# Fused linear attention and GEGLU block: a new partition layout for q, k and v, and kv on quarters of the array

## The chip, the cores and the metric

The kernel runs on one core of a Trainium2 chip. The core has a matrix engine (TensorE, PE in the profile, with PEld for its weight loads), VectorE (DVE), ScalarE (ACT), GpSimd (POOL), SyncE (SP, which issues DMAs) and 16 DMA engines. The metric is device time in microseconds (us). PE writes to PSUM, which has eight banks of 128 x 512 f32; the other engines read the results from there.

## The reference

The inputs are q, k, v of shape 8 x 8 x 576 x 64 (batch, head, token, width) and three weights, all f32.

```python
q_s = softmax(q over the last axis); k_s = softmax(k over the tokens)
kv  = einsum('bhsd,bhse->bhde', k_s, v)            # 64 x 64 per head
o   = einsum('bhsd,bhde->bhse', q_s, kv)
x   = o.transpose(0, 2, 1, 3).reshape(4608, 512)
out = (gelu(x @ w_gate) * (x @ w_val)) @ w_out     # 512 -> 1536 -> 512
```

The kernel takes no maximum off before the exponentials, works in f16 between f32 sums, and divides kv by the sum of exp(k) after the matmul.

## The kernel before, in words

**Layout.** With nine tokens to a group, a head is 64 groups of nine. Partition 2m+t holds group m: for t = 0 tokens 0 to 4, for t = 1 tokens 5 to 8 with an unused slot in front, which is filled once with a value whose exponential is zero (k) or with zero (v). So a tensor of a batch is a tile of 128 partitions x 8 heads x 5 slots x 64, 2560 elements to a partition, of which a tenth is the unused slot. `load` (L180) issues two DMAs for a tensor, one for each t, from SP; in batch 0 the second goes from ACT's queue. `exp` (L223) writes exponentials in f16 as slot x head x width; `cast_v` (L232) makes v f16 and puts a column of ones behind every head.

**Attention of a batch.** `norm_sum` (L241) and `norm_pair` (L250) sum exp(q) over the width on DVE, `norm_mul` (L263) multiplies by the reciprocal on DVE or POOL. q is transposed by PE in batches 0 and 1 (`unit_t`, L391, eight 128x128 transposes for two pairs of heads, twice a batch, copied from PSUM by DVE) and by a DMA from batch 2 on (`unit_td`, L415). kv of a pair of heads is a sum of five matmuls, one for each slot. Batch 1 (`kv_mm`, L304) computes a 128 x 130 block per pair, of which the two blocks off the diagonal are masked away; batch 0 (`kv0_mm`, L340) and the others (`unit_kv4`, L361) compute the two heads of a pair as two matmuls with 64 columns of weights, 40 matmuls a batch. In batch 0 the sums of exp(k) come from matmuls against a column of ones (`ksum_mm`, L327), since k lands before v. x = q_s kv is one 128x128 matmul of 512 columns per pair in batches 0 and 1 (`unit_x`, L438) and eight 64x64 matmuls on quarters of the array in the others (`unit_x4`, L454). The 64 tokens of each batch that don't fit into its 512 are gathered over all batches into a ninth piece of work.

**The block.** Batches 0 and 1 compute twelve slices (fi) of 128 of the 1536 inner columns: four matmuls of 512 columns for gate (psg) and four for val (psv) each, Gelu on ACT, the product on DVE (`ffn_fi`, L520). The first slices are interleaved with the last of the attention (`ffn_first0`, L551; `ffn_first`, L527). The output of batch 0 is plain (`mm_out`, L577, four row tiles, psy). The output of batch 1 (`out_strassen`, L756) and both stages of the rest use Strassen's seven products of half matrices, which need sums of weights and of activations: `sum_w`, `sum_wgv`, `sum_h`, `sum_x`, on DVE and POOL. Weights come through six staging tiles in column chunks (`WCH`, L48), gate and val alternating, and are cast to f16 by POOL (`cast_w`, L209).

**Order.** Every engine and queue executes in program order. For batches 0 and 1 the order is the code's own from L1001 on, with `plan` (L1059) hanging attention steps of the next batch behind slices and output tiles. From batch 2 on it is written out in `PROG` (L675) as words: `0P1` a product, `K` the kv matmuls of the next batch, `k` their normalisation, `X` its x matmuls. PSUM banks go round in a ring (`big`, L81): six and two small ones at first, eight from batch 2 on; a matmul that takes a bank waits for the last reader of it. At the start PE multiplies a constant (`warm_pe`, L500, tile pswarm) until data is there.

Of the kernel before, what the change touches and what calls it, by code (L numbers as in the profile page):

```python
# [18 lines left out]
def kernel(  # L19
# [23 lines left out]
    NM = 4  # L43
    NC = NM + 1
    MAIN = NM * P
    REM = S - MAIN
    VW = D + 1
    WCH = [0, 128, 256] + list(range(512, F + 1, 256))  # L48
    NW = len(WCH) - 1
# [69 lines left out]
    mask = const.tile([P, 2, D], f32)  # L119
# [3 lines left out]
    for i in range(2):  # L123
        eq_b.append(const.tile([P, NC, C], f16, name=f"eq{i}"))
    ek_b.append(const.tile([P, NC, C], f16, name="ek"))
    v16_b.append(const.tile([P, NC, H, VW + 1], f16, name="v16"))
# [5 lines left out]
    eq0r = const.tile([P, C], f16)  # L132
    ld_b = {nm: [const.tile([P, H, NC * D], f32, name=f"{nm}t{i}") for i in range(n)]
# [11 lines left out]
    q0r = [x[0:64].rearrange("p (h d) -> p h d", d=D) for x in (  # L145
        kt1[:, 36 * P:].bitcast(f32), eq_b[1].rearrange("p n c -> p (n c)").bitcast(f32)[:, 1024:])]
# [4 lines left out]
    nc.vector.memset(ld_b["k"][0][:, :, 0:D], -1e30)  # L151
    nc.vector.memset(ld_b["v"][0][:, :, 0:D], 0.0)
    nc.vector.memset(tiny, 0.0)
    nc.vector.memset(ones, 1.0)
    nc.vector.memset(mask, 0.0)
    nc.vector.memset(mask[0:64, 0, :], 1.0)
    nc.vector.memset(mask[64:128, 1, :], 1.0)
    nc.vector.memset(ld_b["q"][0][:, :, 0:D], 0.0)
    make_identity(nc, ident)
    nc.gpsimd.memset(v16_b[0][:, :, :, D:D + 1], 1.0)  # L160
    nc.gpsimd.memset(ld_b["k"][1][:, :, 0:D], -1e30)
# [8 lines left out]
    QUAD = 2  # L170

    def heads(x, b, h0, h1):

        if b >= QUAD:
            return x.rearrange("p (t c) x -> p c t x", t=2)[:, h0 // 2:h1 // 2]
        return x[:, h0:h1]

    tiles = {}

    def load(src, nm, b, h0, h1, n0):  # L180
        tiles[(nm, b)] = buf(ld_b[nm], b)
        for t, c0 in ((0, n0), (1, 1)):
            (nc.scalar if b == 0 and t == 1 else nc.sync).dma_start(  # L183
                out=tiles[(nm, b)][t:P:2, h0:h1, c0 * D:NC * D],
                in_=src[b, h0:h1].rearrange("h (m n) d -> m h (n d)", n=NT)[
                    :, :, (4 * t + c0) * D:(4 * t + NC) * D])

# [6 lines left out]
    def load_w_gv(c):  # L194
        for w, nm in ((moe_w_gate, "wg"), (moe_w_val, "wv")):
            t = wst_tile(f"{nm}st", HP, WCH[c + 1] - WCH[c])
            nc.sync.dma_start(
                out=t, in_=w.rearrange("(ci p) f -> p ci f", p=P)[:, :, WCH[c]:WCH[c + 1]])
            wst[(nm, c)] = t
# [9 lines left out]
    def cast_w(nm, c, eng="pool"):  # L209
        dst = (wg_sb if nm == "wg" else wv_sb)[:, :, WCH[c]:WCH[c + 1]]  # L210
        copy_on(eng, dst, wst[(nm, c)])

    def load_w_o(c):
        t = wst_tile("wost", 2, C)
        nc.sync.dma_start(
            out=t, in_=moe_w_out.rearrange("(fi p) m -> p fi m", p=P)[:, 2 * c:2 * c + 2, :])
        wst[("wo", c)] = t

    def cast_w_o(c, eng="pool"):
        copy_on(eng, wo_sb[:, 2 * c:2 * c + 2, :], wst[("wo", c)])  # L220


    def exp(nm, b, h0=0, h1=H, n0=0):  # L223
        dst = ek_b[0] if nm == "k" else buf(eq_b, b)
        o, i = (("p n (c t d) -> p c t n d", "p c t (n d) -> p c t n d") if b >= QUAD else
                ("p n (h d) -> p h n d", "p h (n d) -> p h n d"))
        nc.scalar.activation(  # L227
            out=dst[:, n0:NC, h0 * D:h1 * D].rearrange(o, d=D, **({"t": 2} if b >= QUAD else {})),
            in_=heads(tiles[(nm, b)], b, h0, h1)[..., n0 * D:NC * D].rearrange(i, d=D),
            func=ACTF.Exp)  # L230

    def cast_v(b, h0, h1, eng="pool"):  # L232
        if h1 - h0 > 2 and (eng == "pool" or b >= QUAD):
            for h in range(h0, h1, 2):
                cast_v(b, h, h + 2, eng)
            return
        copy_on(eng, v16_b[0][:, :, h0:h1, 0:D].rearrange("p n h d -> p h n d"),
                (tiles[("v", b)][:, h0 // 2::4] if b >= QUAD else tiles[("v", b)][:, h0:h1]).rearrange(
                    "p h (n d) -> p h n d", d=D))

    def norm_sum(b, hp, n0=0):  # L241
        n = NC - n0
        e = buf(eq_b, b)[:, n0:NC, hp * P:(hp + 1) * P].rearrange("p n (h d) -> p n h d", d=D)
        rq = att.tile([P, n, 2], f32, name="rq", tag="rq", bufs=4)
        nc.vector.reduce_sum(rq, e, axis=mybir.AxisListType.X)
        rrq = att.tile([P, n, 2], f32, name="rrq", tag="rrq", bufs=4)
        nc.vector.reciprocal(out=rrq, in_=rq)
        st[(b, "norm", hp)] = (e, rrq, n)

    def norm_pair(b, g, n0, engs):  # L250

        n = NC - n0
        e = buf(eq_b, b)[:, n0:NC, 2 * g * P:(2 * g + 2) * P].rearrange("p n (h d) -> p n h d", d=D)
        rq = att.tile([P, n, 4], f32, name="rq2", tag="rq2", bufs=2)
        nc.vector.reduce_sum(rq, e, axis=mybir.AxisListType.X)  # L255
        rrq = att.tile([P, n, 4], f32, name="rrq2", tag="rrq2", bufs=2)
        nc.vector.reciprocal(out=rrq, in_=rq)
        for j in range(2):
            st[(b, "norm", 2 * g + j)] = (e[:, :, 2 * j:2 * j + 2], rrq[:, :, 2 * j:2 * j + 2], n)
        for j, eng in enumerate(engs):  # L260
            norm_mul(b, 2 * g + j, eng)

    def norm_mul(b, hp, eng="dve"):  # L263
        e, rrq, n = st[(b, "norm", hp)]
        (nc.gpsimd if eng == "pool" else nc.vector).tensor_tensor(  # L265
            out=e, in0=e, in1=rrq.unsqueeze(-1).to_broadcast((P, n, 2, D)), op=ALU.mult)

    def norm_mul2(b, hp, cut):
        e, rrq, n = st[(b, "norm", hp)]
        for eng, r in ((nc.vector, slice(0, cut)), (nc.gpsimd, slice(cut, n))):  # L270
            eng.tensor_tensor(out=e[:, r], in0=e[:, r], in1=rrq[:, r].unsqueeze(-1).to_broadcast(
                (P, r.stop - r.start, 2, D)), op=ALU.mult)

    def norm(b, hp, eng="dve", n0=0):
        norm_sum(b, hp, n0)
        norm_mul(b, hp, eng)

    def load_rem0():
        for h0 in (0, 4):
            nc.sync.dma_start(out=q0r[h0 // 4], in_=q[0, h0:h0 + 4].rearrange(  # L280
                "h (m n) d -> m h (n d)", n=NT)[:, :, 0:D])

    def exp_rem0():
        for i in range(2):
            nc.scalar.activation(
                out=eq0r[0:64, i * 4 * D:(i + 1) * 4 * D].rearrange("p (h d) -> p h d", d=D),
                in_=q0r[i], func=ACTF.Exp)

    def norm_rem0():
        e = eq0r[0:64].rearrange("p (h d) -> p h d", d=D)  # L290
        rq = att.tile([64, H], f32, name="rq0", tag="rq0", bufs=1)
        nc.vector.reduce_sum(rq, e, axis=mybir.AxisListType.X)
# [881 lines left out]
```

## Time and profile before

| what | time or share |
|---|---|
| time, median of 3 runs (lowest to highest) | 288.78 us (288.78 to 289.06) |
| profiled execution, first to last instruction | 286.9 us |
| PE busy | 277.9 us, 97% |
| DVE busy | 248.3 us, 87% |
| ACT busy | 209.8 us, 73% |
| POOL busy | 137.9 us, 48% |
| first matmul of the block (psg) starts | 14.96 us |
| slice 2 of batch 0 starts | 19.59 us |
| batch 0's slices end | 36.85 us |
| batch 1's slices end | 70.84 us |
| batch 2's first product starts | 82.11 us |

The profile has the execution's own time as its span alone; the timed median is 1.9 us above the span, for what lies before the first and after the last instruction. All windows and starts are counted from the first instruction. In a timeline a row is a run of equal instructions with its start, its length and, in brackets, how long the engine was idle before it and what ended that. A matmul's row reaches to the modelled end of the last one in it, some 0.2 us after the next row's start, so distances are taken from start to start. The granted PE clock is 1.00 throughout.

### The profile page before, as it was taken

Reading aid. Unit: us, or ns where it says so; the run is one execution under the profiler, and the core shown is the slowest. Engines: PE = TensorE matmul, PEld = TensorE weight load, DVE = VectorE, ACT = ScalarE, POOL = GpSimd, SP = SyncE. Lnnn points to the kernel's source line nnn. Section 1 sums busy time; section 2 is a strip of 40 time slices with the busy share of each in tenths; the row PEclk is TensorE's granted clock in tenths of the full one; section 3 lists DMA queues with packets and bytes.
Section 4 is the critical chain, followed back from the end, with each engine's and each line's share of the span. In section 5 each row is a group of like instructions: output and inputs, shape, how many; then the busy total and the mean of one; then the engine's idle time right before and its main releaser. Section 6 shows DMA issues by size and latency. Waiting matters only on the chain.

```text
span 286.9 us, 6704 instructions
## 1 busy us (share of the span) xinstructions
PE 277.9 (97%) x2581; PEld 216.4 (75%) x2581; DVE 248.3 (87%) x497; ACT 209.8 (73%) x370; POOL 137.9 (48%) x128
## 2 busy tenths in 40 slices
PE   3999999999999999999999999999999999999994
PEld 1544445445888888888888888888888888888883
DVE  2854788877999999979989998999999799998993
ACT  3773367884798889978998899799794577716740
POOL 1557845987339721865864258542553104110110
PEclk9999999999999999999999999999999999999999
DMA  6999999999139916159149853690304030003303
GB/s 215 375 380 386 401 393 390 394 328 243 35 139 339 258 34 223 78 101 321 45 98 308 289 164 150 182 249 2 147 6 90 0 150 0 2 0 77 73 2 146
DMA packets 54623, 51.74 MB, mean 180 GB/s; under 512 B 18496, under 2 KB 50496, under 8 KB 54592
## 3 DMA queue, kind: packets, MB, share of 16 engines
q1 hardware_dynamic: 52864, 49.49, 54.0%
q10 hardware_dynamic: 1728, 1.84, 2.0%
q8 instruction: 20, 0.33, 0.5%
q14 instruction: 11, 0.09, 0.1%
HBM read 37.75 MB, written 9.44 MB: 164 GB/s over the span
## 4 chain that ended last, share of the span: by engine, by line
PE 91%; DVE 5%; ACT 1%; issue 1%; ACTq 1%; DVEq 0%
PE psa L670 24%; PE psc L670 12%; PE psA L749 12%; PE psg L511 7%; PE psv L511 7%; PE psC L749 6%; PE psb L670 6%; PE psy L579 4%; PE psB L749 3%; PE pswarm L503 2%; PE pskv L368 1%; PE psa L749 1%; DVE rq L255 1%; ACTq L183 1%; DVE yo L770 1%
## 5 line engine op out<-in xcount | busy, mean ns | idle before, releaser
L670 PEld LDWEIGHTS <-wgv_sb 128*128 128x128 f16 x672 | 65.7, 98 | 8.0 <-issue 0.3
L265 POOL TENSOR_TENSOR eq<-eq,rrq 128x640 f16<-128x640 f16 (+1 forms) x27 | 34.9, 1303 | 24.3 <-ACT psb L858 11.7
L749 PEld LDWEIGHTS <-ht 128*128 128x128 f16 x384 | 37.2, 98 | 5.3 <-issue 0.4
L670 PE MATMUL psa<-xs,wgv_sb 128*128 128x256 f16 x288 | 40.4, 273 | 0.1
L511 PEld LDWEIGHTS <-wgv_sb 128*128 128x128 f16 x192 | 18.6, 98 | 21.9 <-issue 0.2
L858 ACT COPY psb<-psa 128x512 f32<-128x512 f32 x42 | 24.2, 583 | 8.3 <-PE psa L670 8.1
L511 PE MATMUL psv<-xt,wgv_sb 128*128 128x512 f16 x96 | 26.6, 379 | 0.0
L511 PE MATMUL psg<-xt,wgv_sb 128*128 128x512 f16 x96 | 26.6, 379 | 0.0
L516 ACT ACTIVATE gl<-psg 128x512 f32<-128x512 f32 x24 | 13.8, 597 | 16.7 <-PE psg L511 16.7
L517 DVE SCALAR_TENSOR_TENSOR ht<-psv,gl 128x512 f16<-128x512 f32 x24 | 16.1, 686 | 10.5 <-PE psv L511 8.7
L839 ACT ACTIVATE snq<-psc 128x512 f32<-128x512 f32 x35 | 20.6, 602 | 5.7 <-PE psc L670 5.6
L227 ACT ACTIVATE ek<-kt 128x1280 f16<-128x1280 f32 (+1 forms) x11 | 19.2, 1758 | 5.9 <-DMA kt<-in_k_dram 4.2
L670 PE MATMUL psb<-xt,wgv_sb 128*128 128x256 f16 x144 | 21.6, 273 | 0.0
L670 PE MATMUL psa<-xt,wgv_sb 128*128 128x256 f16 x144 | 21.0, 273 | 0.0
L255 DVE TENSOR_REDUCE rq<-eq 128x20 f32<-128x1280 f16 (+1 forms) x12 | 17.1, 1424 | 4.4 <-ACT eq L227 4.4
L749 PEld LDWEIGHTS <-sh 128*128 128x128 f16 x192 | 18.6, 98 | 2.8 <-issue 0.4
L749 PE MATMUL psA<-tw,ht 128*128 128x256 f16 x168 | 20.6, 272 | 0.0
L227 ACT ACTIVATE eq<-qt 128x2560 f16<-128x2560 f32 (+2 forms) x10 | 18.4, 1861 | 2.6 <-DMA qt<-in_q_dram 2.6
L886 POOL TENSOR_TENSOR ht<-cc 128x512 f16<-128x512 f32 x12 | 15.3, 1274 | 9.1 <-ACT cc L884 8.8
L876 DVE SCALAR_TENSOR_TENSOR ht<-psb,gl 128x256 f16<-128x256 f32 x42 | 17.1, 412 | 1.8 <-ACT gl L874 1.6
L874 ACT ACTIVATE gl<-psa 128x256 f32<-128x256 f32 x42 | 16.1, 385 | 3.4 <-PE psa L670 2.9
L874 ACT ACTIVATE gl<-psb 128x256 f32<-128x256 f32 x42 | 15.5, 382 | 3.8 <-PE psb L670 3.4
(192 smaller groups left out, 694.8 us busy)
## 6 DMA issues: line engine op xcount, KB each, us to landing
out_dram<-yo SPq DMA_DIRECT2D x15, 512.0 KB, 3.5
kt<-in_k_dram SPq DMA_DIRECT2D x7, 640.0 KB, 8.3
vt<-in_v_dram SPq DMA_DIRECT2D x7, 640.0 KB, 7.2
qt<-in_q_dram SPq DMA_DIRECT2D x7, 640.0 KB, 7.0
qt<-in_q_dram SPq DMA_DIRECT2D x8, 512.0 KB, 7.5
wost<-in_moe_w_out_dram SPq DMA_DIRECT2D x6, 512.0 KB, 7.9
kt<-in_k_dram SPq DMA_DIRECT2D x6, 512.0 KB, 7.4
vt<-in_v_dram SPq DMA_DIRECT2D x6, 512.0 KB, 6.6
```

What stands on the lines that cost most here:

```text
L227: nc.scalar.activation(out=dst[:, n0:NC, h0 * D:h1 * D].rearrange(o, d=D, **({"t": 2} if b >= QUAD else {})), in_=heads(tiles[(nm, b)], b, ...
L255: nc.vector.reduce_sum(rq, e, axis=mybir.AxisListType.X)
L265: (nc.gpsimd if eng == "pool" else nc.vector).tensor_tensor(out=e, in0=e, in1=rrq.unsqueeze(-1).to_broadcast((P, n, 2, D)), op=ALU.mult)
L511: nc.tensor.matmul(ps, w[:, ci, fi * P:(fi + 1) * P], xt[:, ci, :], start=(ci == 0), stop=(ci == HP - 1))
L517: nc.vector.scalar_tensor_tensor(out=ht[:, fi, :], in0=psv, scalar=_H_SCALE, in1=gl, op0=ALU.mult, op1=ALU.mult)
L670: nc.tensor.matmul(ps[:, t], a, x, start=(first and t == 0 and c == 0), stop=(c == 1), skip_group_check=True)
L749: nc.tensor.matmul(ps[t], a, w, start=(first and j == js[0] and (t == ts[0] or ps[t].tensor is not ps[ts[0]].tensor)), stop=(j == js[-1]), ...
L839: nc.scalar.activation(out=dst, in_=src, func=ACTF.Copy, scale=scale)
L858: nc.scalar.copy(out=t[f"b{k}"], in_=t[f"a{k}"])
L874: nc.scalar.activation(out=gl, in_=t[ps][:, 1], func=ACTF.Gelu)
L876: nc.vector.scalar_tensor_tensor(out=ht[:, k if x[2] == "2" else k + NO // 2, 0:256], in0=t[ps][:, 0], scalar=_H_SCALE, in1=t["g" + ps], o ...
L886: (nc.vector if side == "dve" else nc.gpsimd).tensor_tensor(out=ht[:, k:k + NO // 2 + 1:NO // 2, 256:512], in0=cc[:, :, 0], in1=cc[:, :, 1 ...
```

## The change

A pair of heads now lies on the two halves of the partitions: partition 64 hh + m holds group m of heads 2a + hh, a = 0 to 3, with all nine tokens: 4 x 9 x 64 = 2304 elements, no unused slot. A tensor is one DMA from SP (batch 0, and k and v of batch 1: two, by halves of a, called j). Exponentials, sums and products go by j or a.

```diff
-    def load(src, nm, b, h0, h1, n0):
+    def load(src, nm, b, j0=0, j1=2, n0=0):
...
-        for t, c0 in ((0, n0), (1, 1)):
-            (nc.scalar if b == 0 and t == 1 else nc.sync).dma_start(
...
+        nc.sync.dma_start(
+            out=tiles[(nm, b)][:, 2 * j0:2 * j1, n0 * D:NT * D],
+            in_=bass.AP(tensor=base.tensor, offset=base.offset + 4 * j0 * S * D + n0 * D,
+                        ap=[[NT * D, P], [2 * S * D, 2 * (j1 - j0)], [1, (NT - n0) * D]]))
...
-    WCH = [0, 128, 256] + list(range(512, F + 1, 256))
+    WCH = [(0, 256, 0, 2), (0, 256, 2, 4), (256, 512, 0, 4), (512, 768, 0, 4)] + [
+        (c, c + 384, r, r + 2) for c in (768, 1152) for r in (0, 2)]
```

The weight chunks are (columns, rows of 128): the first 256 columns come by halves of the rows, the last two 384 columns by halves. The fills of the unused slots and the mask are gone from the start of DVE and POOL.

kv of all batches goes on four 64x64 quarters of the array: the row half is the head of the pair (hh), the column half the slot of the pair (t), and nine tokens are summed. The two row halves write to two PSUM banks, in `unit_kv4` too.

```diff
+    def quarters(j):
+        for hh in range(2):
+            for t in range(2):
+                yield 2 * j + t, hh, t, slice(64 * hh, 64 * hh + 64), slice(64 * t, 64 * t + 64)
...
+    def kv_mm(b, j):
+        for n in range(NT):
+            for a, hh, t, r, o in quarters(j):
+                nc.tensor.matmul(st[(b, "pskv")][hh][o, j, 0:D], ek_b[0][r, n, a * D:(a + 1) * D],
+                                 v16_b[0][r, n, a, 0:D], start=(n == 0), stop=(n == NT - 1))
...
+    def x_mm(b, j, ps, src):
+        for a, hh, t, r, o in quarters(j):
+            nc.tensor.matmul(ps[t][r], st[(b, "kv")][o, hh, j, :], src(b, j, t, hh), start=True, stop=True)
```

`ksum_mm` is 36 such matmuls of one column per j, `unit_kv` (batch 1) and `unit_kv4` 72 of 65 columns a batch. x of batches 0 and 1 is `x_mm`, eight quarter matmuls of 512 columns instead of four full ones. `t_mm` and `t_out` are the transposes and their copy. `kv_norm` scales by the reciprocal, one row half on DVE and one on ACT; `kv4_norm` takes two reciprocals and two products instead of one each.

The start of batch 0 and the slices of batches 0 and 1:

```diff
-    warm_pe(15)
-    unit_t(0, 0, None)
...
+    warm_pe(14)
+    t_mm(0, 0)
+    kv_banks(0)
+    ksum_mm(0, 0)
+    t_out(0, 0, "act")
+    ksum_rec(0, 0)
+    cast_vn(0, 0, (0, 3, 6, 9), ("dve", "act", "pool"))
     warm_pe(3)
...
+    ksum_mm(0, 1)
+    ksum_rec(0, 1)
+    t_mm(0, 1)
+    kv_mm(0, 0)
+    t_out(0, 1, "dve")
+    kv_norm(0, 0, ("dve", "act"))
+    cast_vn(0, 1, (0, 3, 6, 9), ("dve", "act", "pool"))
+    unit_x(0, 0, True)
+    kv_mm(0, 1)
...
+    first = [((L(kv_norm, 0, 1, ("dve", "dve")), L(unit_x, 0, 1, True), L(preload, ACTF.Gelu)), ()),
+             ((), ())]
...
+            ffn_first(xt, (0, 1), first[b])
...
+                for fis in ((2, 3), (4, 5), (6, 7, 8), (9, 10, 11)):
+                    ffn_group(xt, fis)
```

The new `ffn_first` runs, for slices 0 and 1, gate and then val on rows 0 and 1, what `first` holds between them, and then rows 2 and 3. The new `ffn_group` runs the gate of all slices of a group and then their val. In the queue of SP, k and v of batch 1 come as k, k, v, v, and the second half of the last chunk of w_out behind them. In batch 0's output the last slice (11) of all four row tiles comes after slices 0 to 10 of all four, and the attention of batch 1 hangs there:

```diff
+    at(0, NS, 15, L(t_mm, 1, 1), L(t_out, 1, 1, "dve"), L(cast_vn, 1, 0, (0, 4, 9), ("dve", "act")))
+    at(0, NS, 16, L(cast_vn, 1, 1, (0, 4, 9), ("dve", "act")),
+       L(load_batch, 2, ((v, "v"),)))
+    at(0, NS, 17, L(kv_banks, 1), L(unit_kv, 1), L(cast_w_o, 5, "pool", 1, 2))
+    at(0, NS, 6, L(unit_x, 1, 0, True), L(unit_x, 1, 1, False, ()), L(sum_w, 3, "pool"))
+    at(0, NS, 8, L(x_out, 1, 1), L(sum_w, 1), L(sum_w, 2, "pool"), L(exp, "q", 2), L(preload, ACTF.Gelu))
...
-    at(1, NS, 2, L(sum_wgv, "g", 3), L(sum_wgv, "v", 3))
+    at(1, NS, 0, L(sum_wgv, "g", 3, 0, NO // 2, "pool"), L(sum_wgv, "v", 3, 0, NO // 2, "pool"))
```

Two sums of weights (`sum_wgv`, 3) thus move from DVE to POOL in batch 1's output. `PROG` is unchanged; only its words' contents shrink from 2560 to 2304 elements a tensor.

## The prediction

> **What bounds the kernel now.** First the page's head and its table of busy time.
>
> ```profile
> span 286.9 us, 6704 instructions
> ...
> PE 277.9 (97%) x2581; PEld 216.4 (75%) x2581; DVE 248.3 (87%) x497; ACT 209.8 (73%) x370; POOL 137.9 (48%) x128
> ```
>
> PE is busy 97% of the span. Second, the table by stage (length, busy time and count of PE, PEld, DVE, ACT, POOL, then clock, DMA share, GB/s), since 97% of the whole does not say where the rest lies.
>
> ```profile
> 14.96:19.59 4.63, 4.63 (x35) 1.93 (x30) 1.88 (x5) 3.73 (x7) 3.17 (x4) 1.00 1.09 383
> ...
> 70.84:82.11 11.27, 11.12 (x151) 9.09 (x149) 11.07 (x23) 8.93 (x9) 3.36 (x4) 1.00 0.23 84
> 82.11:287.00 204.89, 200.96 (x2052) 176.14 (x2050) 187.58 (x386) 158.52 (x307) 87.34 (x76) 1.00 0.42 127
> ```
>
> From 19.59 on PE has nothing to wait for: the psg and psv rows follow each other by 0.86 us per four matmuls (0.216 each), products of 256 columns by 1.31 per twelve (0.109 each). The one exception is batch 1's output, 70.84 to 82.11, where DVE is busy 11.07 of 11.27. So time can be won in three places: before 19.59, in PE's own work, and in that output. Third, the chain of waits at the start, and ACT's timeline under it.
>
> ```profile
> 4.91 5.95 PE pswarm L503 x15
> ...
> 13.16 0.34 PE pskv L346 x10
> ...
> 15.03 0.32 PE psg L511
> ...
> 19.59 0.86 PE psg L511 x4
> ```
>
> ```profile
> 6.52 2.00 ACT L227 ACTIVATE eq<-qt 128x1024 f16<-128x1024 f32 x2 [1.67 <-DMA qt<-in_q_dram]
> 10.02 2.43 ACT L227 ACTIVATE ek<-kt 128x1280 f16<-128x1280 f32 x2 [1.50 <-DMA kt<-in_k_dram]
> 12.57 1.45 ACT L205 CAST v<-vt 128x320 f16<-128x320 f32 x3
> ...
> 17.31 1.28 ACT L506 ACT_TABLE_LOAD   x1
> ```
>
> ACT waits for the whole of q, then of k, then of v: the start is bound by transfers. Fourth, PE's timeline around kv and x, for what a quarter of the array costs.
>
> ```profile
> 45.56 0.74 PE L309 MATMUL pskv<-v,ek 128*128 128x130 f16 x10
> 46.13 1.03 PE L579 MATMUL psy<-wo_sb,ht 128*128 128x512 f16 x4
> ...
> 101.69 0.82 PE L368 MATMUL pskv<-v,ek 128*64 128x65 f16 x40
> 102.45 0.50 PE L749 MATMUL psB<-wo_sb,ht 128*128 128x256 f16 x3
> ...
> 106.48 0.26 PE L462 MATMUL psxr<-eqt,kv 64*64 64x64 f16 x8
> 106.56 0.60 PE L462 MATMUL psx<-eqt,kv 64*64 64x512 f16 x8
> 107.10 1.26 PE L749 MATMUL psC<-wo_sb,s 128*128 128x256 f16 x10
> ```
>
> From start to start, batch 2's kv holds PE 0.76, one half of batch 1's 0.57, eight quarter matmuls of 512 columns 0.54, eight of 64 columns 0.08. Eight times 512 columns one by one would be 8 x 0.216 = 1.73: four quarters run together.
>
> **The change, part by part.** The sum is made against the profiled span of 286.9; the runs' median of 288.78 is 1.9 above it, and I add the same.
>
> *Start of batch 0.* The bytes of q, k, v are the same, but come in order by halves. ACT's half of q (0.52 MB) landed 4.4 us after its issue at 0.73, so q's first half is there at 5.1, the second at 6.4 (SP's half took 5.7). At 0.386 MB/us (5 to 12.4 us) each further 0.59 MB takes 1.53: k at 7.9 and 9.5, v at 11.0 and 12.5. That one queue starts as fast as two is not shown; if it doesn't, up to 0.5 is lost, and rows of 2304 bytes instead of 1024 and 1280 may win as much (402 GB/s were moved from 37 to 40 us, with rows up to 2 KB). I take neither. SP issues six DMAs of 0.8 (its rows are 0.76 to 0.92), done by 5.5, ahead of the transfers; the weights queue behind them as before. ACT is freed of three issues, so its table load and the warm-up start 2 us sooner. ACT then does exp q 5.1 to 6.2 (1.0 each), exp q 6.4 to 7.5, exp k (1152 elements, 1.15 from the 1.27 for 1280) 7.9 to 9.1 and 9.5 to 10.7, the transposed q (1024 elements, 1.0 as for exp) to 11.7, its third of v (0.46, as for 320 elements) to 12.2. DVE's sums, reciprocals and products (1.22 + 0.25 + 0.69 after each exp q) are done by 10.6, POOL's two products of 1.5 by 11.5, both ahead of ACT. So kv starts at 12.2 instead of 13.16. Its nine steps, kv's scaling (0.35 before, taken the same), x (0.4) and the copy (0.59, behind ACT's third of v's second half) put the first psg at 14.3 instead of 14.96. From there to slice 2 before took 4.63: sixteen matmuls (3.45), two x, two kv. After, it is sixteen matmuls and one x by quarters, 0.5 with its switch of array mode: 18.3. There slice 2's gate needs the bank of slice 0's, whose Gelu waits for the copy of x, the table load (1.28 + 0.20) and itself (0.60): 18.4. **-1.2.**
>
> *Weights.* Nobody waits for them now. Slice 4's gate weights are the tightest:
>
> ```profile
> 20.94 1.04 POOL L203 CAST wgv_sb<-wgst 128x1024 f16<-128x1024 f32 x1 [1.58 <-DMA wgst<-in_moe_w_gate_dram]
> ```
>
> They are cast at 21.98; after, PE wants them at 18.4 + 3.45 = 21.85, with the same bytes ahead. The chunks of 512-byte rows are gone (347 GB/s from 12.4 to 15.0 against 385 after it), which brings 0.3. So nothing is lost here, with 0.2 to spare; without that cover 0.1 is. The later groups need larger chunks at once (0.79 MB, 2.0 us, cast in two parts of 0.8), but their group of three gives PE 5.2 us for 4.0 of transfers.
>
> *Batch 1's attention.* PE's work: kv 2 x 0.57 becomes 0.70 (below), x 4 x 0.216 = 0.86 becomes 0.54: -0.75. The price is late work. PE reaches kv at 36.85 - 1.2 + 44 x 0.216 + 0.9 for the transposes = 46.0. The last transfer of v, issued at 41.1, landed at 47.1 before (6.0); k, k, v, v with half a w_out chunk moved behind (0.26 MB, 0.65 us), the 0.3 from above and a cast of 0.7 (640 elements) on two engines at once put v at 46.2 landed, 46.9 cast; larger rows could bring 0.8. PE waits 0 to 0.9: I take 0.4. Behind that wait stand slice 11 of the output, for which its weights come another 0.65 + 0.61 (a 512-element cast) after v's landing, 47.5, and x. Then x's copies (0.59, 0.69) come before batch 1's first psg, with only one row tile (0.22) to cover them: 0.5. Last, ACT has two copies, exp q of batch 2 (2.1, from 2.34) and the table load (1.5) before batch 1's first Gelu, now at 54.26; PE will have filled its six banks by 54: 0.1. Sum -0.75 + 1.0 = **+0.25**; ends -0.7 and +1.2.
>
> *Batch 1's output.* Of the 11.27 us, 84 matmuls of 256 columns (9.2), kv (0.76) and x (0.8) are 10.8: 0.5 is lost to DVE. Two sums of 0.82 leave DVE for POOL, which is busy 3.36 there (on POOL 512 elements take 1.15, so 768 some 1.7 each), and the sums of exp(q) before it shrink. **-0.4**; ends 0 and -0.5.
>
> *kv of batches 2 to 7.* Now 20 pairs in 0.76, 0.038 a step with the switch. After: 18 steps of four. Bounds for a step: 0.038, as now, or half of the 0.08 that eight quarters of 64 columns took, 0.04, and at worst two at a time, 0.076. I take the first, 0.70: -0.06 x 6 = **-0.35**. At worst 1.37, +0.6 a batch. `kv4_norm` costs DVE two instructions (0.17 and 0.42 at most) more; PE doesn't wait for them, since x comes after several other words.
>
> Here stands a rule against this change. "TensorE: Matmul & The Clock Gate" of the Trainium skill (Wait — 56ns, not 53.3ns?) says that two matmuls never start less than about 25 ns apart, however few columns they have. By it 72 would hold PE 1.8 us and 40 matmuls 1.0, some +6 over the run. Eight quarters began within 0.08 and 40 half-array ones within 0.76, 10 and 19 ns each, so the measurement decides: that floor is not one per quarter.
>
> *A second bank for kv.* K holds two of eight banks until k instead of one. Nearest row: PE's longest wait for a bank from 82 on, 0.27 at 118. Ends 0 and 0.3 x 6 = 1.8. At each K two or more banks are free in the ring, so I take 0.
>
> *The rest.* exp, sums, products and casts shrink by a tenth, the DMA transposes too. All lie beside PE, as the last stage row shows, so nothing is won; should ACT or DVE cover less, nothing gets longer.
>
> *The clock.* PE goes at half speed until some 5 us into the warm-up (matmuls of pswarm last 631 ns, then 376, though the granted clock reads 1.00). After, the warm-up ends at 8.6 and PE has gaps until 14.3, of under 1 us each. Ends: 0, or 3.4 at half speed, +1.7. I take 0. The same page (The two states you'll see) says the clock falls after an idle window of some 3.4 us; no gap here is so long, so by the rule too it is 0.
>
> Sum: -1.2 + 0.25 - 0.4 - 0.35 = -1.7. 288.78 - 1.7 = **287.1**.
>
> **The rivals.** (A) *The quarters of kv do not overlap four at a time*, for they accumulate over nine steps, which no quarter matmul of before does. +0.6 x 6, +0.6 for batch 1 and as much at the start: +4.8 on -1.7: 291.9, slower. It decides from a step of 0.052 on (18 x 0.014 x 7 = 1.7). For it: no such row exists. Against: pairs that accumulate in L368 do overlap, and quarters of L462 do. (B) *The banks*: +1.8 on -1.7, 288.9, no change. (C) *Transfers*: v and w_out of batch 1 come when they came, and PE gives back the start: only the output's and kv's 0.75 stay, 288.0. DMA is saturated to 55 us, which speaks for it; that w_out's half is moved speaks against. (D) *The transfers run at 0.404*, so v lands 0.5 sooner at the start and 0.8 sooner in batch 1, and no wait is left: 285.6. (E) *The clock* falls or the one queue starts slowly: 288.6.
>
> **How the numbers follow.** Forecast 0.50, A 0.12, B 0.11, C 0.09, D 0.12, E 0.06. The measurement tells 0.2% (0.6 us) from no change. Faster: forecast 0.47, D 0.12, C 0.07, B and E 0.05, 0.71. Slower: A 0.12 and 0.06 from B and E, 0.18. Same: 0.11. The range takes in D and B, and half of what A can be at a step somewhat above 0.052: 285.2 to 289.4. The forecast's own range is 286.2 to 288.1.
>
> **What would show it.** The first psg near 14.3, slice 2 near 18.4; 72 pskv within 0.75 from start to start; PE idle around 46 to 49 with v or kv's scaling as the reason; no 0.76 for x in batch 1's output; from 82 on the same distance from batch 2's first product to the end, less 0.3. Wrong if pskv takes over 0.95, if PE waits for banks around K, or if weights hold slices 4 to 8.

## The result: 355.8 us instead of 288.8

The changed kernel takes 355.78 us (median, 355.10 to 356.64), the kernel before 288.80 beside it. The ratio is 1.232, with a 95% interval of 1.230 to 1.234: 67 us slower, where 287.1 was predicted. Executions over 1.5% longer than the fastest of the same kernel are left out of all times: one of e1_store16's four and three of e6_sums_dve's ten, its profiled one among them.

The page of the kernel after; in the clock, DMA and GB/s rows each digit or number is one fortieth of the span, 8.9 us:

```profile
span 354.9 us, 7334 instructions
...
PE 289.6 (82%) x2913; PEld 221.1 (62%) x2913; DVE 250.8 (71%) x492; ACT 208.6 (59%) x373; POOL 138.0 (39%) x130
...
PEclk9789999998999699989997799958998999999955
...
GB/s 251 386 372 372 408 341 159 67 151 342 169 172 181 210 24 57 64 319 32 99 281 166 147 30 183 51 199 7 53 64 67 18 54 48 5 118 0 26 52 42
```

PE was busy for 97% of the span and is for 82% of it; in microseconds it works 12 us more, since its granted clock is 0.61 to 0.93 in the stages below, where before had 1.00. The last two numbers of the GB/s row, 52 and 42, stand where PE has nothing left to do. No engine became the bound. The table by stage says where it waits (columns as in the prediction: length, busy time and count of PE, PEld, DVE, ACT, POOL, then clock, DMA share and GB/s):

```profile
15.26:21.16 5.90, 5.90 (x21) 1.96 (x20) 1.32 (x5) 3.16 (x5) 3.79 (x6) 0.64 1.08 385
...
74.37:88.11 13.74, 11.41 (x169) 8.64 (x168) 11.32 (x19) 7.13 (x7) 5.10 (x3) 0.88 0.88 290
88.11:331.90 243.79, 211.49 (x2223) 181.45 (x2223) 191.43 (x399) 158.18 (x307) 87.68 (x80) 0.93 0.53 104
331.90:354.90 23.00, 0.27 (x3) 0.00 (x0) 0.42 (x1) 0.03 (x1) 0.00 (x0) 0.61 0.12 45
```

The end of before, cut in the same way:

```profile
282.91:286.94 4.03, 0.27 (x3) 0.00 (x0) 0.42 (x1) 0.02 (x1) 0.00 (x0) 0.96 0.55 205
```

The same stages side by side, cut at the same events in three traces (the third is the first experiment below). All cuts are starts in PE's timeline; by it slice 2 of before starts at 19.43, which its chain of waits puts at 19.59:

| stage | before | after | e1_store16 |
|---|---|---|---|
| up to the first psg | 14.96 | 15.26 | 14.70 |
| to slice 2 of batch 0 | 4.47 | 5.90 | 4.05 |
| rest of batch 0's slices | 17.26 | 17.27 | 17.26 |
| batch 0's output, batch 1's attention and slices | 33.99 | 35.94 | 34.50 |
| batch 1's output up to the product behind x | 9.96 | 13.74 | 12.28 |
| from there to the last matmul's start | 202.27 | 243.79 | 202.18 |
| from there to the end | 4.03 | 23.00 | 5.07 |

Of the 68 us between the two spans, 41.5 lie in the batches from 2 on, where the prediction saw a gain of 0.35, and 19.0 behind the last matmul, which it did not mention. The list of waits of the kernel after names what PE and ACT wait for there (us in total, times, longest):

```profile
PE psxr L381 <- DMA eqt<-eq: 20.6, 4, 9.0
...
ACT eq L212 <- DMA qt<-in_q_dram: 19.6, 5, 10.0
...
ACT eq L212 <- DMA eqt<-eq: 16.1, 2, 11.6
...
PE psb L584 <- ACT psb L772: 9.5, 1, 9.5
```

All four are one story: PE needs the transposed q for x, ACT needs the next q and the buffer that the transposition reads, and PE's banks wait for ACT. The list of before has no wait of PE for a DMA. SP's timeline, which shows how long SP was held at each DMA (start, length), says what is ahead of the transpositions. After:

```profile
53.18 1.71 SPq L503 DMA_DIRECT2D out_dram<-yo  x2
54.95 10.84 SPq L353 DMA_TRANSPOSE eqtr<-eq  x1
...
72.08 11.35 SPq L360 DMA_TRANSPOSE eqt<-eq  x1
```

and before:

```profile
50.10 0.67 SPq L589 DMA_DIRECT2D out_dram<-yo  x1
50.81 2.48 SPq L411 DMA_TRANSPOSE eqtr<-eq  x1
...
62.62 4.24 SPq L418 DMA_TRANSPOSE eqt<-eq  x1
```

A stretch of the kernel after while a store is under way:

```profile
57.00:65.00 8.00, 8.00 (x39) 3.63 (x37) 6.23 (x10) 6.50 (x10) 4.71 (x4) 1.00 0.15 55
```

The DMA share is 0.15 and the rate 55 GB/s, though a transposition waits on the queue all that time: one eighth of the sixteen engines is 0.125. Between 331.90 and the end it is 0.12 and 45 GB/s. In the first stretch the trace has some 12 packets of 4096 bytes per us, of 0.17 us each, which is two engines at work. What carries these stores is an edit of one line, which the prediction did not cost:

```diff
     def store(eng, src, b, n0, n1, c0=0, c1=C):
...
-                                  ap=[[pm, nm], [NM * pn, 2]] + last), in_=src)
+                                  ap=[[(NT - 1) // 2 * pn, 2], [pm, nm]] + last), in_=src)
```

The new layout puts the row tile's two halves of 64 tokens one behind the other on the partitions, so the outer dimension of the store is 2 instead of 64. The trace has it as a shape of 64 x 2 instead of 2 x 64 (inner first).

The lines that answer to the others shown of before. ACT at the start, and POOL's cast of slice 4's gate weights:

```profile
5.69 1.06 ACT L212 ACTIVATE eq<-qt 128x1024 f16<-128x1024 f32 x1 [0.51 <-DMA qt<-in_q_dram]
9.01 1.16 ACT L212 ACTIVATE ek<-kt 128x1152 f16<-128x1152 f32 x1 [2.26 <-DMA kt<-in_k_dram]
```

```profile
20.76 1.04 POOL L189 CAST wgv_sb<-wgst 128x1024 f16<-128x1024 f32 x1 [0.28 <-DMA wgst<-in_moe_w_gate_dram]
```

q came earlier than predicted (second half 5.7 instead of 6.4), k a microsecond later (9.0 instead of 7.9). And PE around batch 1's kv:

```profile
48.91 0.48 PE L306 MATMUL pskv<-v,ek 64*64 64x65 f16 x36
51.32 0.48 PE L306 MATMUL pskv<-v,ek 64*64 64x65 f16 x36 [1.93 <-DVE v L193]
```

### The profile page after: what moved, and what is told of

It is laid out like the page before. It is cut to its first block, busy times and chain, and to the rows that moved or that the text cites. A ratio compares the mean times of both kernels' runs of the same rounds, so it can differ in the third digit from the quotient of the medians.

```text
span 354.9 us, 7334 instructions
## 1 busy us (share of the span) xinstructions
PE 289.6 (82%) x2913; PEld 221.1 (62%) x2913; DVE 250.8 (71%) x492; ACT 208.6 (59%) x373; POOL 138.0 (39%) x130
## 4 chain that ended last, share of the span: by engine, by line
PE 38%; DMA 23%; ACT 1%; issue 1%; DVE 0%; SPq 0%; ACTq 0%
DMA eqt<-eq 18%; PE psa L584 14%; PE psc L584 8%; PE psA L663 7%; DMA qt<-in_q_dram 5%; PE psC L663 4%; PE psb L584 4%; PE psB L663 1%; ACT eq L212 1%; PE psx L381 0%; ACT psb L772 0%; PE psxr L381 0%; ACT gl L753 0%; ACT xt L191 0%; SPq L167 0%
## 5 line engine op out<-in xcount | busy, mean ns | idle before, releaser
L584 PEld LDWEIGHTS <-wgv_sb 128*128 128x128 f16 x672 | 66.1, 98 | 18.6 <-issue 10.2
L238 POOL TENSOR_TENSOR eq<-eq,rrq 128x576 f16<-128x576 f16 (+1 forms) x28 | 34.4, 1244 | 42.5 <-ACT psb L772 27.4
L212 ACT ACTIVATE eq<-qt 128x2304 f16<-128x2304 f32 (+2 forms) x10 | 17.1, 1721 | 35.7 <-DMA qt<-in_q_dram 19.6
L436 PEld LDWEIGHTS <-wgv_sb 128*128 128x128 f16 x192 | 19.1, 100 | 24.0 <-issue 2.8
L230 DVE TENSOR_REDUCE rq<-eq 128x18 f32<-128x1152 f16 (+1 forms) x16 | 21.1, 1321 | 12.7 <-ACT eq L212 12.7
L436 PE MATMUL psg<-xt,wgv_sb 128*128 128x512 f16 x96 | 24.6, 390 | 0.4 <-ACT xt L191 0.4
L436 PE MATMUL psv<-xt,wgv_sb 128*128 128x512 f16 x96 | 24.5, 389 | 0.0
L663 PE MATMUL psA<-tw,ht 128*128 128x256 f16 x168 | 21.7, 281 | 0.0
L212 ACT ACTIVATE ek<-kt 128x1152 f16<-128x1152 f32 (+1 forms) x11 | 17.7, 1605 | 5.3 <-DMA kt<-in_k_dram 3.1
L381 PE MATMUL psxr<-eqt,kv 64*64 64x64 f16 x48 | 1.9, 215 | 20.6 <-DMA eqt<-eq 20.6
L572 POOL TENSOR_TENSOR xs<-xt,xs 128x512 f16<-128x512 f16 x6 | 6.9, 1152 | 28.8 <-DVE xs L572 24.9
```

The lines of the kernel that those rows point to most:

```text
L212: nc.scalar.activation(out=dst[:, n0:NT, j0 * P:j1 * P].rearrange("p n (a d) -> p a n d", d=D), in_=tiles[(nm, b)][:, 2 * j0:2 * j1, n0 * ...
L238: (nc.gpsimd if eng == "pool" else nc.vector).tensor_tensor(out=e, in0=e, in1=rrq.unsqueeze(-1).to_broadcast((P, n, D)), op=ALU.mult)
L436: nc.tensor.matmul(ps, w[:, ci, fi * P:(fi + 1) * P], xt[:, ci, :], start=(ci == 0), stop=(ci == HP - 1))
L572: (nc.gpsimd if eng == "pool" else nc.vector).tensor_tensor(out=o, in0=a, in1=b, op=ALU.subtract)
L584: nc.tensor.matmul(ps[:, t], a, x, start=(first and t == 0 and c == 0), stop=(c == 1), skip_group_check=True)
L663: nc.tensor.matmul(ps[t], a, w, start=(first and j == js[0] and (t == ts[0] or ps[t].tensor is not ps[ts[0]].tensor)), stop=(j == js[-1]), ...
```

## The experiments

Two theories stand at the start. S: the stores go by two engines, everything behind them on the queue waits, and that is the 65 us. T: the new transpositions of eighteen blocks, or rows of 2304 bytes on a single queue, are slow in themselves. K, as a third: the clock alone.

**e1_store16: the same stores with an outer dimension of 64.**

```diff
-        eng.dma_start(out=bass.AP(tensor=base.tensor, offset=base.offset,
-                                  ap=[[(NT - 1) // 2 * pn, 2], [pm, nm]] + last), in_=src)
+        for u in range(2):
+            eng.dma_start(out=bass.AP(tensor=base.tensor, offset=base.offset + u * (NT - 1) // 2 * pn,
+                                      ap=[[pm, nm]] + last), in_=src[64 * u:64 * u + 64])
```

> The kernel after, with each output store written as two DMAs, one for each half of the partitions, whose outer dimension is 64 rows instead of 2 halves; everything else as it is. Theory S (the stores, whose outer dimension is 2, are carried by two of the sixteen DMA engines, and the DMA transposes and loads behind them on the same queue wait): no packets of 4096 bytes at 13 per us any more, the issue of the eqt transposes back from 11 us to 3 to 6, the wait of PE for them gone, the distance from the last matmul to the end back from 22.5 to about 4 us, the granted clock back to 0.97 or more; the time is the prediction of 287.1 plus what the start (1.9) and batch 1's wait for v (2.0) cost, 288 to 292. Rival T (the transposes of eighteen blocks, or rows of 2304 bytes on one queue, are slow in themselves): the issue of the transposes stays near 11 us, only the last 19 us go, and the time stays at 335 to 352. Rival K (the clock alone): the clock stays at 0.91 and the time above 345.

Measured: 291.90 us (291.83 to 292.69), ratio 1.0115 to before (1.0095 to 1.0135). The stages of its profile:

```profile
14.70:18.75 4.05, 4.05 (x21) 1.58 (x20) 1.19 (x5) 2.61 (x5) 2.85 (x5) 1.00 1.09 380
...
70.51:82.79 12.28, 9.92 (x170) 7.78 (x168) 11.16 (x20) 7.03 (x7) 7.63 (x7) 1.00 0.12 42
82.79:284.97 202.18, 202.04 (x2223) 177.24 (x2223) 188.33 (x399) 157.53 (x307) 84.55 (x76) 1.00 0.43 124
284.97:290.04 5.07, 0.28 (x3) 0.00 (x0) 0.42 (x1) 0.03 (x1) 0.00 (x0) 1.00 0.65 180
```

63.9 us are gone with this edit alone, transpositions and rows as they were: S holds and T and K fall. The clock is 1.00 again, so its fall from batch 1's output on was a result of the waits. (In the kernel after it also falls once before any store, from 12.72 to 19.54; of that below.) The transposition that held SP for 11.35 us holds it for 2.67:

```profile
63.65 2.67 SPq L360 DMA_TRANSPOSE eqt<-eq  x1
```

What is left, 3.1 us more than before by the two profiles, sits in two rows of the stage table above all: batch 1's output (+2.3) and the end (+1.0).

**e2_before_store2 and e3_store8: two tries that changed nothing.** In e2 the kernel before had its outer dimension of 64 written as two of 32; in e3 the halves had theirs written as eight of eight.

```diff
-                                  ap=[[pm, nm], [NM * pn, 2]] + last), in_=src)
+                                  ap=[[nm // 2 * pm, 2], [pm, nm // 2], [NM * pn, 2]] + last), in_=src)
```

> The kernel before, with its output stores' access pattern split so that the outer dimension is 2 instead of 64; the same bytes go to the same rows in the same number of DMAs, and nothing of the rest of the change is in it. Theory S: 4096-byte packets at some 13 per us, transposes that wait 9 to 17 us behind a store, some 18 us more at the end, and 335 to 360 us. Rival T: only the end grows, 300 to 310 us. Rival K: no more than 291 us.

In e3, on e1_store16's lines:

```diff
-                                      ap=[[pm, nm]] + last), in_=src[64 * u:64 * u + 64])
+                                      ap=[[8 * pm, 8], [pm, nm // 8]] + last), in_=src[64 * u:64 * u + 64])
```

> The kernel after, with each store as two DMAs as in e1_store16, but with an outer dimension of 8: a dose between 2 and 64. Theory S: a 512 KB store takes a quarter of the 10 us that it takes at 2, about 2.5 us, twice that at 64; the time is 0 to 4 us above that of e1_store16, so 288 to 296. If instead the number of DMAs (two for one) were what matters, it equals e1_store16 to 0.5 us. Rivals T and K: as in e1_store16, 335 or more.

Measured: 288.80 and 291.54 us (one execution each), the times of before and of e1_store16. In both traces the DMAs carry the old shape (2 x 64; 64 x 1): adjacent dimensions whose steps continue each other are merged into one, so neither kernel tested its dose. Both are repeats and count for nothing else.

**e4_tail16: the last batch's stores alone.**

```diff
+        if b < B - 1:
+            eng.dma_start(out=bass.AP(tensor=base.tensor, offset=base.offset,
+                                      ap=[[(NT - 1) // 2 * pn, 2], [pm, nm]] + last), in_=src)
+            return
+        for u in range(2):
...
```

The lines behind the loop's head are those of e1_store16.

> The kernel after, with the stores of the last batch alone written as in e1_store16. It tells how much of the loss is the drain behind the last matmul and how much is in the waits before it. Theory S: from the last matmul to the end 4 us instead of 22.5, the rest as it was: 334 to 340 us. If the last stores wait for those of the batch ahead of them in the queue, some of the 18 us stays, and it is 340 to 350.

Measured: 336.24 us (one execution), 5.4 us of them behind the last matmul's start. So 19.5 us of the loss are the drain of the last stores, and the 44 us that are left to e1_store16 are waits before it: here PE still waits 22.8 us for the transpositions.

**e5_before_store2p: the stores' edit alone, in the kernel before.** The two outer dimensions are exchanged; in this order they are not merged (the trace has 64 x 2). The rows of the output come out in another order for it.

```diff
-                                  ap=[[pm, nm], [NM * pn, 2]] + last), in_=src)
+                                  ap=[[NM * pn, 2], [pm, nm]] + last), in_=src)
```

> The kernel before, with the two outer dimensions of its stores exchanged, so that the outer one is 2 and the two can't be merged into one of 64, as they were in e2_before_store2; the same bytes leave, in the same number of DMAs, but the rows of the output are in another order than the reference's. Nothing of the rest of the change is in it. Theory S (an outer dimension of 2 means two of the sixteen engines): 4096-byte packets at some 13 per us, a wait of PE for the eqt transposes of several us per batch, some 18 us more behind the last matmul, and 335 to 360 us. Rival T (it takes the new transposes and row lengths as well): the end grows by 18, the waits do not, 300 to 310 us. Rival: the stores are not the cause at all, 288.8 us.

Measured: 358.12 us (one execution), 69 above before. Its list of waits and its last stage repeat those of the kernel after, with none of its other edits:

```profile
PE psxr L462 <- DMA eqt<-eq: 25.2, 5, 7.9
```

```profile
333.24:356.33 23.09, 0.27 (x3) 0.00 (x0) 0.42 (x1) 0.03 (x1) 0.00 (x0) 0.61 0.12 44
```

With e1_store16 this closes the main question from both sides: the edit is enough to lose the time, and undoing it is enough to get it back.

**m1_moves: the stores by themselves.** Eighteen stores of 512 KB one after the other, three of each pattern, and sixteen loads ahead of them.

```diff
...
+            if kind == "o64":
+                rows(r, [[W, 64], [64 * W, 2]])
+            elif kind == "halves":
+                for u in range(2):
+                    rows(r + 64 * u * W, [[W, 64]], s[64 * u:64 * u + 64])
+            else:
+                n = int(kind[1:])
+                rows(r, [[W, n], [n * W, P // n]])
```

> A kernel of transfers alone, which computes nothing of the reference and writes zeros to all rows of the output: sixteen loads of a q or k of 1.18 MB, one after the other, in batches 0, 2, 4, 6 with rows of 2304 bytes as after loads them and in batches 1, 3, 5, 7 with rows of 1280 and 1024 bytes as before does (there as two DMAs), and then eighteen stores of 512 KB, one after the other: three each with an outer dimension of 64 over 128 partitions (as before), as two DMAs of 64 partitions (as in e1_store16), and with an outer dimension of 2 (as after), 4, 8 and 16. Theory S: from issue to landing some 3 us at 64, and 10 us at 2 (two engines at 159 ns for each of 64 packets), so 5 to 6 at 4, 3 to 4 at 8, and no more at 16 than at 64. For the halves: if 64 partitions are slower in themselves (packets of 0.30 us in e1_store16's end against 0.16 in before's), 1 us or more above the store at 64; if those packets were long for what else went on there, the same as at 64 but for a second issue of 0.6. For the loads: if rows of 2304 bytes are slower in themselves (some packets of 0.8 to 1.6 us at 5 us in the kernels with them, none above 0.06 after 3 us in before), their loads take longer by 0.5 us or more in every batch; if that is only so at the start of a program, the first alone; if not, 1.18 MB take 3 us and the 2 us of a single transfer's delay in both.

Measured, on the third of each (windows from the first packet's start to the last one's end: length, busy DVE and POOL, clock, DMA share, GB/s), in the order in which they ran:

```profile
161.81:163.24 1.43, 0.00 (x0) 0.00 (x0) 1.00 0.91 367
166.02:168.19 2.17, 0.00 (x0) 0.00 (x0) 1.00 0.93 242
171.04:182.32 11.28, 0.00 (x0) 0.00 (x0) 1.00 0.13 46
185.14:193.60 8.46, 0.00 (x0) 0.00 (x0) 1.00 0.21 61
196.45:200.75 4.30, 0.00 (x0) 0.00 (x0) 1.00 0.45 121
203.59:205.74 2.15, 0.00 (x0) 0.00 (x0) 1.00 0.88 240
```

These are 64, halves, 2, 4, 8 and 16. The share of busy engines follows the outer dimension: 0.13, 0.21, 0.45, 0.88 for 2, 4, 8, 16 against 2/16, 4/16, 8/16, 16/16. So the dose is there: 11.3, 8.5, 4.3, 2.1 and 1.4 us. (4 and 8 were expected faster, at 5 to 6 and 3 to 4 from issue to landing, and 16 no slower than 64.) "DMA: Bandwidth & Descriptors" of the Trainium skill, in "Why a DMA increments its semaphore by 16 and not by 1", states this as a rule: a DMA runs on the largest number of engines up to 16 that divides the outermost dimension of both of its access patterns. The busy shares of the runs agree, and the rule gives 2 for the changed line at first reading.

The second row is news: two DMAs of 64 partitions keep the engines just as busy (0.93), but their packets of 4096 bytes take 0.25 us in the mean instead of 0.16, and 512 KB take 2.17 us instead of 1.43. "SBUF — State Buffer" of the skill (Door 1: The DMA port swizzle) has DMA bandwidth depend on how many of 16 ports the partitions reach. That would fit the halves, but it is not shown to be the cause: the stores with an outer dimension of 8 and 16 leave from all 128 partitions, and their packets are as long (0.24 us in the mean). In e1_store16's end the two halves come with more issues and longer packets (0.27 us for those of 4096 bytes), and it is 1.0 us longer; what each of the two costs was not separated. The loads ran beside each other in this kernel and tell nothing of rows of 2304 bytes.

**e7_before_sums_pool: the two sums alone, in the kernel before.** This and the next settle batch 1's output, where the prediction had a gain. In e1_store16 POOL's two sums and DVE's rows beside them:

```profile
71.50 4.13 POOL L557 TENSOR_TENSOR wgv_sb<-wgv_sb 128x768 f16<-128x768 f16 x2
```

```profile
72.61 1.53 DVE L541 TENSOR_TENSOR s<-ht,sh 128x1024 f16<-128x1024 f16 x1
74.06 1.85 DVE L541 TENSOR_TENSOR sh<-ht 128x512 f16<-128x512 f16 x1
```

```profile
75.98 0.61 PE L664 MATMUL psc<-tw,sh 128*128 128x256 f16 x4 [1.81 <-DVE sh L541]
```

In before the same two rows of DVE took 0.67 and 0.41. But before had the same thing once, a little earlier, where a DVE sum of 1024 elements ran beside a POOL sum and took 1.53 too:

```profile
69.40 1.53 DVE L626 TENSOR_TENSOR sh<-sh,ht 128x1024 f16<-128x1024 f16 x1
```

```profile
68.78 1.60 POOL L651 TENSOR_TENSOR wgv_sb<-wgv_sb 128x512 f16<-128x512 f16 x1
```

The single edit:

```diff
-    at(1, NS, 2, L(sum_wgv, "g", 3), L(sum_wgv, "v", 3))
+    at(1, NS, 0, L(sum_wgv, "g", 3, 0, NO // 2, "pool"), L(sum_wgv, "v", 3, 0, NO // 2, "pool"))
```

> The kernel before, with only its two sums over 768 elements moved to POOL at the place where the kernel after has them. Theory P: DVE's f16 sums beside them get longer as in e1_store16, 2.0 to 2.4 us above before: 290.8 to 291.3 us. The prediction's own term: 0.4 below, 288.4. Rival Q: 288.5 to 289.

Measured: 290.64 us, ratio 1.0060 (1.0043 to 1.0076): 1.7 us slower, a little less than expected. The rows repeat it:

```profile
71.72 1.52 DVE L626 TENSOR_TENSOR ht<-ht 128x1024 f16<-128x1024 f16 x1
...
73.77 1.53 DVE L626 TENSOR_TENSOR s<-ht,sh 128x1024 f16<-128x1024 f16 x1
```

Its stage of batch 1's output is 11.54 us instead of 9.96. DVE's rows on f32 from PSUM (ht, 0.68) are not touched by POOL in either trace; its sums of two f16 tiles are.

**e6_sums_dve: the sums back on DVE, in e1_store16.** The same edit the other way round.

```diff
-    at(1, NS, 0, L(sum_wgv, "g", 3, 0, NO // 2, "pool"), L(sum_wgv, "v", 3, 0, NO // 2, "pool"))
+    at(1, NS, 2, L(sum_wgv, "g", 3), L(sum_wgv, "v", 3))
```

> e1_store16 with the two sums over 768 elements of batch 1's output put back on DVE, at the place where the kernel before has them. Theory P (while POOL runs these sums of 2.07 us each, DVE's own f16 sums are held up: 1.53 us for 1024 elements instead of 0.67, 1.85 for 512 instead of 0.41, and PE waits 1.97 and 0.62 for them): PE's waits at batch 1's output go back to 0.2 and 0.5, and the time is 2.0 to 2.3 below e1_store16's, 289.8 to 290.4 us. The prediction's own term (the move wins 0.4): 0.4 above e1_store16's, 292.7. Rival Q (DVE is late there for another reason, such as the four instructions of kv's scaling): no change, 292.3.

Measured: ratio 1.0033 to before (1.0016 to 1.0049), 289.8 us, against 1.0115 for e1_store16: 2.4 us won. In its trace DVE's two rows take 0.68 and 0.42 again. P holds from both sides, and with the stores and these sums repaired the kernel is still 1 us slower than before.

**e8_all, e9_best, e10_no_warm: is there a version that beats both?** e8_all adds to e6_sums_dve a split of the very last store over SP and ACT, later first transposes in batch 1, and seven more warm-up matmuls.

```diff
...
-    warm_pe(14)
+    warm_pe(17)
     t_mm(0, 0)
     kv_banks(0)
+    warm_pe(4)
...
-    at(0, NS, 3, L(t_mm, 1, 0), L(t_out, 1, 0, "dve"))
+    at(0, NS, 14, L(t_mm, 1, 0), L(t_out, 1, 0, "dve"))
```

> e6_sums_dve with three small edits: the second half of the very last store is issued by ACT instead of SP; the first transposes of batch 1 stand ten slots later, where POOL's product (41.7 us in e1_store16) is long done; and 3 + 4 more warm-up matmuls fill PE's gaps of 0.78 and 1.08 us before and after the first transposes. Expected: 0.5 less behind the last matmul, 0.4 less in batch 0's output, and nothing for the warm-up where the matmuls of slice 0 run at 0.216 anyway (1.9 less where they run at 0.43): 288.6 to 289.5 us, the same as before to 0.2%. If the added warm-up matmuls delay what follows, 289.5 to 290.

Measured: ratio 1.0040 (1.0025 to 1.0055), 290.0 us; not told from e6_sums_dve, and above the 288.6 to 289.5 that were expected. Its trace has the reason: the end stays at 5.0 us, since the last store is issued 0.5 us sooner but its packets end only 0.1 sooner, and what PE loses to POOL's product of exp(q) (start to start, less the matmul's own time) moved from the first transposes, 0.60 in e1_store16, to the second, 0.82.

e9_best puts one of the two sums on POOL behind the casts of v, where POOL has 5 us free, moves the second transposes a slot too, and stores row tile 3 of the last batch in one piece; e10_no_warm is the same without the seven warm-up matmuls. The main lines of e9_best that differ from e8_all's (the second `t_mm` of batch 1 went from `at(0, NS, 15, ...)` to 16):

```diff
-    at(1, NS, 2, L(sum_wgv, "g", 3), L(sum_wgv, "v", 3))
+    at(1, NS, 2, L(sum_wgv, "g", 3, 0, NO // 2, "pool"), L(sum_wgv, "v", 3))
...
+    at(0, NS, 16, L(t_mm, 1, 1))
...
-        store(nc.sync, yo[:, 1, 256:], b, 3, 4, 256, 512)
...
-        store(nc.scalar, yo[:, 0], b, 2, 3)
+        store(nc.scalar, yo[:, 0], b, 2, 3, split=True)
...
-        store(nc.sync, yo[:, 1, 0:256], b, 3, 4, 0, 256, True)
+        store(nc.sync, yo[:, 1], b, 3, 4, split=True)
```

> e8_all with four things changed after what its trace shows: one of the two sums of batch 1's output runs on POOL, but behind POOL's casts of v (free there from 79.95 to 85.30 us in e8_all), the other stays on DVE; the second transposes of batch 1 stand one slot later, since PE waited 0.82 us there for POOL's product; row tile 3 of the last batch leaves as one row of 2048 bytes instead of two of 1024, and the last two stores are split over SP and ACT. Expected against e8_all: 0.7 less for DVE's yo (1.13 us waited there), 0.8 less before the second transposes, up to 0.6 less at the end: 287.8 to 288.6 us, below before by 0.1 to 0.3%. If v's arrival takes the place of the transposes' wait, 0.5 of it is lost: 288.3 to 289.

> e9_best without the seven added warm-up matmuls. If the matmuls at half their rate at the start (0.43 us each in the trace of after, 0.216 in e1_store16 and e8_all) come from PE's gaps of 0.8 to 1.4 us behind the warm-up, then some of its runs lie 1.5 to 4 us above the others, as in e1_store16 (291.83 to 296.36), and those of e9_best do not; the fast ones lie within 0.3 of e9_best. If the gaps have nothing to do with it, both scatter alike.

Measured: e9_best 289.57 us (288.42 to 292.05), ratio 1.0026 (1.0006 to 1.0045); e10_no_warm 290.17 (288.66 to 292.11), ratio 1.0044 (1.0026 to 1.0062). 287.8 to 288.6 was expected of e9_best. In its profile the last matmul begins at 281.44, 1.5 us earlier than before's, but the end takes 5.20 instead of 4.03; batch 1's output, with one sum on POOL behind the casts, takes 9.98, as long as before's 9.96. It is the closest in ratio, though its interval overlaps that of e6_sums_dve, and slower than before in the median. Both scatter by 3.5 us where before scatters by 0.5, so the length of the warm-up is not what makes the scatter. No version here beats the kernel before. A store that keeps all 128 partitions and an outer dimension of 64, by writing x's two halves in turns on neighbouring partitions, would need no second DMA; it was not tried.

## Why the prediction was wrong

**The step that failed is "The rest".** It named exponentials, sums, casts and the transpositions, "all lie beside PE", and so costed at 0 whatever it did not list. The line in `store` fell under that and was not read as a change of cost: the access pattern writes the same bytes to the same rows. It measured +63.9 us (after against e1_store16), +69 alone. The sentence that the DMA transposes lie beside PE had a condition, that their queue is free ahead of them; SP carries them behind the stores, and of these the prediction said nothing. None of the five rivals had it either: C and D asked when loads come, not what a store holds up. The end of the trace of before had a hint: 4.0 us behind the last matmul's start, in which nothing but stores is left.

The other terms can be read on e1_store16, whose stores are repaired:

- *Start of batch 0, -1.2:* -0.26 to the first psg and -0.42 to slice 2, -0.68. The right sign and mechanism (kv begins at 12.4 instead of 13.16, one x by quarters replaces two x and a kv), too large above all by the arrival of k: 8.8 instead of 7.9. The prediction counted two kv behind the first psg of before; the trace has one of ten matmuls there (16.60), the other begins ahead of it (14.69).
- *Weights, 0 with 0.2 to spare:* right in e1_store16, but the tight place is slice 2 and not slice 4, whose cast ends 1.2 ahead of its use there. In e10_no_warm slice 2 waits 0.57 for POOL's cast of its weights.
- *Batch 1's attention, +0.25:* +0.51. PE loses 0.60 to POOL's product before the first transposes, which the sum did not have, and 0.40 to x's copy; the wait for v is not there. In the kernel after it is 1.95; there the cast of v met POOL's sum of w_out, as these rows say, and took 3.80 us for what took 0.85 in e1_store16:

```profile
47.47 3.80 DVE L193 CAST v<-vt 128x512 f16<-128x512 f32 x2
```

```profile
47.84 3.14 POOL L521 TENSOR_TENSOR tw<-wo_sb 128x1536 f16<-128x1536 f16 x1
```

- *Batch 1's output, -0.4:* +2.3. This step took the two sums' 1.64 us off DVE and let POOL do them for nothing, since POOL was idle. The row of before at 69.40 (shown at e7) was not read. The runs show DVE's f16 sums ending just behind POOL's instruction: the one that starts at 74.06 in e1_store16 ends at 75.91, POOL's pair at 75.63. "SBUF — State Buffer" of the skill ("SBUF: two separate sides") has this as an exclusive lock: of a DVE operation with two inputs from SBUF and a GpSimd one that reads SBUF, the first to start has the shared pair of ports for its whole length. The measurement agrees, f32 rows from PSUM being free of it.
- *kv of batches 2 to 7, -0.35:* the mechanism is right, the gain half as large. From start to start 72 matmuls took 0.71 in four batches of e1_store16 and 0.76 in the other two, against 0.76 for the 40 before; 0.70 was predicted for all six. (The row of before that the prediction calls batch 2's, at 101.69, is batch 3's; batch 2's takes as long.) Rival A is refuted: the accumulating quarters run four at a time.

```profile
103.84 0.78 PE L320 MATMUL pskv<-v,ek 64*64 64x65 f16 x72
104.55 1.48 PE L664 MATMUL psB<-wo_sb,ht 128*128 128x256 f16 x12
```

- *A second bank for kv, 0:* right; in the whole of e1_store16's last stage PE is idle for 0.14 us of 202.18. Rival B is refuted.
- *The clock, 0 with an end of +1.7:* right in e1_store16 (1.00), at the wrong end in the kernel after's profile: 0.64 in the stretch to slice 2, which took 5.90 instead of 4.05. That end, a part of rival E, was +1.7, and it is 1.85. The first slice's rows of after and of e1_store16:

```profile
15.26 1.86 PE L436 MATMUL psg<-xt,wgv_sb 128*128 128x512 f16 x4 [0.19 <-ACT xt L191]
```

```profile
14.70 1.02 PE L436 MATMUL psg<-xt,wgv_sb 128*128 128x512 f16 x4 [0.27 <-ACT xt L191]
```

The granted clock of after is 0.50 from 12.72 to 19.54. PE's longest gap behind the warm-up is 1.20 us there, with a late k, and 0.91 in e1_store16. Whether the longer gap is the cause is not shown; e4_tail16, whose code is the same up to there and whose longest gap is 0.62, kept its clock, and so did e10_no_warm with 0.82. The rule that the prediction cited from "TensorE: Matmul & The Clock Gate" (an idle window of some 3.4 us) does not explain the fall.

So with the stores repaired -1.7 was predicted and +2.1 measured up to the last matmul, then +1.0 for the end. The sign would still have been wrong, by batch 1's output (+2.3, the two sums on POOL) and the end.

## What to carry to other kernels

Read the outer dimension of every DMA that a change touches, stores too, as a number of engines, and cost a DMA by what stands behind it on its queue, not by who waits for its data. An idle POOL is not a free place for f16 sums while DVE has f16 sums on the path; behind them, as in e9_best, it was. In a diff, list the lines that the cost did not use; a line that is neutral for the bytes can be the whole result.

## What was not expected of the hardware

- A store of 512 KB by two engines takes 11.3 us alone (46 GB/s), against 1.43 by all (367 GB/s), and holds the transpositions queued behind it, which hold SP for 11 us instead of 2.5 to 4.2.
- Two stores from 64 partitions each have packets of 0.25 us where one from 128 has 0.16, with the engines equally busy (0.93 and 0.91). Stores from 128 partitions with an outer dimension of 8 or 16 have them of 0.24 as well; the cause is open.
- The loads of rows of 2304 bytes are unsteady in their first microseconds. In the stretch from 4 to 8 us the rate and what follows are:

| kernel | GB/s, 4 to 8 us | first exp(k) starts | first psg |
|---|---|---|---|
| before | 386 | 10.02 | 14.96 |
| e7_before_sums_pool | 387 | 10.24 | 15.15 |
| after | 301 | 9.01 | 15.26 |
| e4_tail16 | 330 | 8.38 | 14.30 |
| e1_store16 | 382 | 8.83 | 14.70 |
| e9_best | 395 | 7.74 | 14.09 |
| e10_no_warm | 324 | 8.63 | 14.60 |

With the old rows and two queues no packet between 4 and 8 us took over 0.2 us; with the new ones the longest of each trace takes 0.7 to 1.6. The scatter of the repaired versions fits this, as everything up to batch 1 hangs on these transfers, but what makes the packets long, the rows or the single queue, stays open.
